# Two edits of a fused forward and backward kernel: block 3 of the first norm turned by DMA, and one pair of loads held on an earlier product

## Chip, cores and metric

The kernel runs on one core of a Trainium2 chip. The metric is the device time of one execution in microseconds (us): the median of several executions, lower is better. All times of single instructions below come from one profiled execution.

## The reference, cut to what matters

Four residual layers, A, B, A, B (numbered l = 0 to 3 in the kernel), and then the gradients of all six inputs by reverse differentiation. S = 2048 rows, D = 512, 32 heads of 16, F = 1376, everything in bfloat16.

```
x = x + A(layernorm(x));  x = x + B(layernorm(x));  x = x + A(layernorm(x));  x = x + B(layernorm(x))
A: q, k, v = h @ wqkv;  pq, pk = phi(q), phi(k)                  # phi(t) = t + 1 where t > 0, else exp(t)
   kv = sum over s of pk^T v;  z = sum over s of pk;  o = (pq @ kv) / (pq . z);  return o @ wo
B: return (sigmoid(h @ w_gate) * (h @ w_up)) @ w_down
outputs: x and the gradients of x, wqkv, wo, w_gate, w_up, w_down
```

The edits touch the layernorm in front of the first layer A (l = 0) and the backward pass of both layers A (l = 2, which comes first, and l = 0, which comes last).

## The kernel before

**Tiling.** The 2048 rows are 16 tiles of 128 rows (`st`), four to a block (`b` = 0 to 3, `j` the tile in the block). Each tile of x stays in SBUF through the whole program. A matmul contracts over partitions, so most stages need the rows both as they are (`h`) and turned (`hT`, features on partitions).

**The first norm** is `LN.one` for l = 0 (L276 to L298). For each tile it takes the statistics on DVE and POOL, writes `h` on DVE (L288), turns it with four TensorE transposes against the identity into a PSUM bank `T_ps` (L292), and copies the bank to `hT` on ScalarE: one tile at a time in block 0 (L296), two tiles at a time in blocks 1 to 3 (L298). At the end of a block `h` is stored from POOL's queue (L317), and `hT` is put on a list of stores for SP's queue (L319, L221). The later norms (l = 1 to 3) turn their rows by DMA transposes from SBUF to SBUF on SP's queue (L314).

**The stage around it** is `AFwd.first` (L483). It walks over the 16 tiles: it asks the norm to be six tiles ahead (L501), computes the keys of a later tile (`keys`, L464: `k_ps` on TensorE from `hT`, then ScalarE and DVE make `pk_t`), for some tiles a pair of query products from a block's `hT` (`query`, L522), and then the sums `E_ps` (L512, from `h` and `pk_t`) and `z_ps` (L515). `hT` of tiles 12 and 13 is first read by the thirteenth key product, that of tiles 14 and 15 by the fifteenth. Finished pairs of `pk_t` are turned by DMA transposes on SP (L478); the weights of layer B are loaded on SP, each held on a certain `pk_t` (L425 to L429).

**The backward of a layer A** is `a_bwd1` and then `a_bwd2`. `a_bwd1` (L1021) has per block b: four products `dq_ps` (L1071) from the turned gradient `gaT_t`, each followed by two "fill" products, DVE and POOL work (`soft`, L1049), and sixteen sums `CT_ps` (L1046) that read `qn_l` of the block. The inputs of block b come from DRAM over SP's queue: `loads(b)` are two loads of 512 KB (`qp_l` L1035 and `dqT_t` L1036), `rows_n(b)` is one (`qn_l` L1041). `loads(0)` and `rows_n(0)` are written first, `loads(1)` is held on the last of twelve fill products (L1063, L1064), and the later ones on a ScalarE copy of the block before (L1083).

**The fill** (`Fill`, L227) is a weight gradient of layer 3 that is cut into 11 groups of 16 products (L250) and put in wherever TensorE would wait. The input of a group is one DMA transpose of 512 KB from DRAM (`hf_t`, L238); two buffers take turns, and the load of the next group is written ahead of a group's fourth product. The last-but-one `a_bwd1` (l = 2) starts with product 0; the last one (l = 0) starts with the sixteenth product of group 7, so that the load for group 9 is written ahead of its fifth product, and its buffer comes free with its first.

**Order.** The program is written in one order; a planner then gives each engine, and each engine's DMA queue, an order of its own: what its estimate says is ready goes first, and among what is ready, what was written first. An engine's queue is then worked off strictly in that order. So in the trace the load of group 1 of the fill is issued at 493.39 us, ahead of loads that were written before it (501.64 us). `held` adds a wait; it does not place the instruction.

Of the kernel before, what the change touches and what calls it, by code (L numbers as in the profile page):

```python
# [22 lines left out]
NDC = D // P  # L23
# [23 lines left out]
def by_tile(ap2d, st, n):  # L47
    return ap2d[rows(st, n), :].rearrange("(n p) d -> p n d", p=P)


def by_chunk(ap2d, b):

    return ap2d[:, b * SB:(b + 1) * SB].rearrange("(c p) s -> p c s", p=P)
# [101 lines left out]
def flat(t):  # L155
    return t[:].rearrange("p a b c -> p (a b c)") if len(t.shape) == 4 else t[:].rearrange("p a b -> p (a b)")
# [37 lines left out]
def mm4(k, out, lhs, rhs, n=NDC):  # L194
    for c in range(n):
        i = k.nc.tensor.matmul(out, lhsT=lhs(c), rhs=rhs(c), start=(c == 0), stop=(c == n - 1))  # L196
    return i


def after(k, second, first, cls=None):  # L200

    k.tc.add_manual_dep(second.ins, first.ins.name,
                        mybir.DependencyInfo(cls or mybir.DependencyClass.NoSync, mybir.DependencyReason.DATA),
                        reason="order")


def held(k, first, *loads):
    for ld in loads:
        after(k, ld, first, mybir.DependencyClass.Sync)


def store_turned(k, dst, t):

    flush_turned(k)
    k.turned.append((dst, t))
# [47 lines left out]
class LN:  # L263
# [12 lines left out]
    def one(self, st):  # L276
        k, nc, l = self.k, self.k.nc, self.l
        b, j = divmod(st, NB)
        if j == 0:
            self.h[b] = k.p_h.tile([P, NB, D], BF16, name="h_t", tag="h_t")  # L280
            self.hT[b] = k.p_hT.tile([P, NB, NDC, P], BF16, name="hT_t", tag="hT_t")
        if l == 0:
            if st == 0:
                self.stats(0)
            if st + 1 < NST:
                self.stats(st + 1)
            mean, rstd = self.got.pop(st)
            self.applied.append(nc.vector.tensor_scalar(self.h[b][:, j, :], narrow(k, st), mean, rstd, ALU.subtract, ALU.mult))  # L288
            if j % 2 == 0:
                self.tp = k.bank([P, 2 * NDC, P], BF16, name="T_ps")  # L290
            for c in range(NDC):
                t = nc.tensor.transpose(self.tp[:, j % 2 * NDC + c, :], self.h[b][:, j, c * P:(c + 1) * P], k.ident[:])  # L292
                if st == 2 and c == 0:
                    after(k, t, k.last_key)
            if b == 0:
                nc.scalar.copy(self.hT[b][:, j], self.tp[:, j % 2 * NDC:j % 2 * NDC + NDC, :])  # L296
            elif j % 2:
                nc.scalar.copy(self.hT[b][:, j - 1:j + 1].rearrange("p a c q -> p (a c) q"), self.tp[:])  # L298
        elif j % 2:

            rstd = k.rstd[l][:, st - 1:st + 1]
            neg = k.small.tile([P, 2], F32, name="ln_neg", bufs=8)
            nc.scalar.mul(neg[:], k.sums[st // 2][:], -1.0 / D)
            ss = k.small.tile([P, 2], F32, name="ln_ss")
            for i in range(2):
                nc.scalar.activation(self.h[b][:, j - 1 + i, :], k.xs[st - 1 + i][:], ACT.Square, bias=neg[:, i:i + 1],
                                     accum_out=ss[:, i:i + 1])
            nc.gpsimd.tensor_scalar(rstd, ss[:], 1.0 / D, EPS_LN, ALU.mult, ALU.add)
            nc.gpsimd.tensor_tensor(rstd, rstd, k.neghalf[:], ALU.pow)
            for i in range(2):  # L310
                nc.vector.tensor_scalar(self.h[b][:, j - 1 + i, :], k.xs[st - 1 + i][:], neg[:, i:i + 1],
                                        rstd[:, i:i + 1], ALU.add, ALU.mult)
            if b or l == 2:
                nc.sync.dma_start_transpose(out=self.hT[b][:, j - 1:j + 1].rearrange("p a c q -> p (a c) q"),  # L314
                                            in_=self.h[b][:, j - 1:j + 1, :].rearrange("p a d -> p (a d)"))
        if j == NB - 1:
            k.st.dma_start(out=by_tile(k.sv[l]["h"], b * NB, NB), in_=self.h[b][:])  # L317
            if l % 2 == 0:
                store_turned(k, k.sv[l]["hT"][b], self.hT[b])  # L319
# [25 lines left out]
def narrow(k, st):  # L345

    return k.xs[st][:].bitcast(BF16)[:, D:2 * D]
# [673 lines left out]
def a_bwd1(k, l, big, ph1, p_dq):  # L1021
    nc, sv, A = k.nc, k.sv[l], k.A[l]
    MT = k.p_mt.tile([P, NDC, D], BF16, name="MT_l", tag="MT")
    nc.sync.dma_start(out=flat(MT), in_=k.wT[4 if l else 5][:])
    dzp = big.tile([P, NDC, NBLK], F32, name="dzp")
    CT_ps = [k.bank2([P, D], F32, name="CT_ps") for _ in range(NDC)]
    late, gs, dqTs, qps, qns = [], k.early, [], [], {}

    def loads(b):

        if b % 2 == 0:
            qps.append(k.p_sh.tile([P, 2, NDC, SB], BF16, name="qp_l", tag="sh"))
        dqTs.append(p_dq.tile([P, NDC, SB], BF16, name="dqT_t"))
        half = NDC * SB
        lds = (nc.sync.dma_start(out=flat(qps[-1][:, b % 2]), in_=sv["qr"][b][:, 0:half]),  # L1035
               nc.sync.dma_start(out=flat(dqTs[b]), in_=sv["qr"][b][:, half:2 * half]))  # L1036
        return lds

    def rows_n(b):
        qns[b] = big.tile([P, NDC, NB, P], BF16, name="qn_l", tag=f"big{b % 2}")  # L1040
        return nc.sync.dma_start(out=flat(qns[b]), in_=sv["qn"][b])  # L1041

    def sums(b, g_t, qn):
        for jc in range(NDC):
            for j in range(NB):
                nc.tensor.matmul(CT_ps[jc][:], lhsT=g_t[:, j, jc * P:(jc + 1) * P], rhs=qn[:, :, j, :],  # L1046
                                 start=(b == 0 and j == 0), stop=(b == NBLK - 1 and j == NB - 1))

    def soft(b, dc, dq, u_t, qp, dqT):  # L1049
        t_ps = k.bank([P, SB], F32, name="t_ps")  # L1050
        nc.tensor.matmul(t_ps[:], lhsT=k.bdmask[:], rhs=u_t[:], start=True, stop=True)
        w_t = ph1.tile([P, SB], BF16, name="w_t", bufs=3)
        nc.vector.scalar_tensor_tensor(w_t[:], t_ps[:], A["nz"][:, dc:dc + 1], dq[:], ALU.mult, ALU.add)
        nc.gpsimd.tensor_tensor(dqT[:, dc, :], w_t[:], dqT[:, dc, :], ALU.mult)
        nc.vector.scalar_tensor_tensor(u_t[:], t_ps[:], -1.0, qp[:, dc, :], ALU.mult, ALU.mult,
                                       accum_out=dzp[:, dc, b:b + 1])
        if dc == NDC - 1:
            k.st.dma_start(out=by_chunk(sv["dqT"], b), in_=dqT[:])

    loads(0)  # L1060
    rows_n(0)
    gs.append(a_grads(k, 2))
    k.fill.step(12)  # L1063
    held(k, k.fill.last, *loads(1))  # L1064
    for b in range(NBLK):
        g_t, gT = gs[b]
        qp, dqT = qps[b // 2][:, b % 2], dqTs[b]
        qn = qns[b]
        for dc in range(NDC):
            ps = k.bank([P, SB], F32, name="dq_ps")  # L1070
            mm4(k, ps[:], lambda c: MT[:, c, dc * P:(dc + 1) * P], lambda c: gT[:, :, c, :])  # L1071
            dq = ph1.tile([P, SB], BF16, name="dq_sb", bufs=3)
            k.mark = nc.scalar.copy(dq[:], ps[:])
            u_t = ph1.tile([P, SB], BF16, name="u_t", bufs=3)
            nc.vector.tensor_tensor(u_t[:], dq[:], qp[:, dc, :], ALU.mult)
            late.append((b, dc, dq, u_t, qp, dqT))
            k.fill.step(2)
            if len(late) > 2:
                soft(*late.pop(0))
            if (b, dc) == (0, 1):  # L1080
                gs.append(a_grads(k, 3))
            if dc == 1 and b + 1 < NBLK:
                held(k, k.mark, rows_n(b + 1), *(loads(b + 2) if b + 2 < NBLK else ()))  # L1083
                if b == 1 and l == 2:
                    held(k, k.mark, nc.sync.dma_start(out=flat(k.woT), in_=k.wT[0][:]),
                         *(nc.sync.dma_start(out=flat(k.wqkvT[:, NDC * i:NDC * i + NDC, :]), in_=k.wT[1 + i][:])
                           for i in range(3)))
        sums(b, g_t, qn)
    while late:
        soft(*late.pop(0))  # L1090


    CT = big.tile([P, NDC, D], BF16, name="CT_t", tag="big0")
    for jc in range(NDC):
        nc.scalar.copy(CT[:, jc, :], CT_ps[jc][:])
    k.st.dma_start(out=sv["CT"][:].rearrange("(c p) d -> p c d", p=P), in_=CT[:])
    return CT, dzp, dqTs
# [246 lines left out]
```

## Time and profile before

| | |
|---|---|
| median of 4 executions | 1090.32 us (1088.72 to 1092.0) |
| the profiled execution | 1092.0 us, of them 1090.3 us from the first to the last instruction |
| TensorE busy | 1062.0 us, 97% of the span |
| DVE, ScalarE, POOL busy | 51%, 41%, 28% |
| first norm's transposes on TensorE (L292) | 64, 7.4 us busy, 5.8 to 35.4 us |
| copies of two turned tiles on ScalarE (L298) | 6, 1010 ns each |
| DMA transposes of key pairs, 256 KB (L478) | 16; to landing 3.1, 4.4, 8.5 us (least, median, most) |
| loads qp_l, dqT_t, qn_l, 512 KB each | to landing 6.4, 7.2, 6.3 us (median) |
| fill loads hf_t, 512 KB, turned | 11; to landing 7.2 us (median) |
| l = 2 `a_bwd1` | its products start at 501.45 us |
| l = 0 `a_bwd1` | its products start at 738.95 us |

How to read it: TensorE is busy nearly all of the span, so a wait of TensorE is the place where time can be gained or lost, and the other engines and the queues count where they make TensorE wait. In a timeline of an engine, a line gives the start, the duration, the engine, the source line, the operation, what it writes and reads, how often, and in brackets how long the engine had stood idle and what ended it. The start of TensorE's next line is the better measure of a matmul's cost, since matmuls overlap. "SPq" is SP's queue, whose instructions only issue DMAs.

### The profile page before, as it was taken

The page shows a single profiled execution, that of the slowest core. Times are in us where ns is not written, and L with a number is a line of the kernel's source. Part 1 is how long each engine was busy: PE and PEld are TensorE (multiplying, and loading weights), DVE is VectorE, ACT ScalarE, POOL GpSimd, SP SyncE. Part 2 cuts the span into 40 slices and gives each one's busy share as a digit, 9 for nine tenths or more (in the row PEclk, how much of TensorE's full clock was granted, in tenths as well). Part 3 has the DMA queues.
Part 4 walks back from the last instruction along what each step waited for, and adds up shares of the span by engine and source line. Part 5 has one row for each costly group of instructions (what it writes and reads, how often), then busy time and mean ns, then how long its engine had stood idle before and what let it go on. Part 6 is the DMA issues. An engine that isn't in the chain of part 4 may idle for free.

```text
span 1090.3 us, 15262 instructions
## 1 busy us (share of the span) xinstructions
PE 1062.0 (97%) x5448; PEld 495.0 (45%) x5448; DVE 551.4 (51%) x1029; ACT 444.9 (41%) x930; POOL 306.5 (28%) x410
## 2 busy tenths in 40 slices
PE   6989999999999999999899999999999999999998
PEld 3444444444444444444344444444444444465443
DVE  7687765668935443545676534557877100001110
ACT  3477686448736464533234533434336100000010
POOL 5334443104643434231532200003623200001110
PEclk9999999999999999999999999999999999999999
DMA  9988988679999999899997888869989996499991
GB/s 270 274 230 274 293 220 246 190 191 256 269 237 221 261 185 271 193 221 210 340 312 214 233 274 240 238 184 251 355 233 341 259 248 154 123 213 237 260 223 41
DMA packets 401869, 258.50 MB, mean 237 GB/s; under 512 B 308720, under 2 KB 371472, under 8 KB 400512
## 3 DMA queue, kind: packets, MB, share of 16 engines
q1 hardware_dynamic: 386608, 208.12, 77.2%
q0 software_dynamic: 15184, 49.39, 13.0%
q8 instruction: 43, 0.70, 0.3%
q14 instruction: 34, 0.28, 0.1%
HBM read 76.19 MB, written 106.79 MB: 168 GB/s over the span
## 4 chain that ended last, share of the span: by engine, by line
PE 68%; DMA 2%; ACT 1%; DVE 1%; issue 1%; POOL 1%; SPq 0%; ACTq 0%; DVEq 0%; POOLq 0%
PE dw_ps L1288 19%; PE dh_ps L848 7%; PE dh_ps L942 7%; PE dhh_ps L196 6%; PE dh_ps L1127 5%; PE y_ps L196 4%; PE dw_ps L1306 3%; PE u_ps L196 3%; PE g_ps L196 3%; PE dh_ps L1118 3%; PE dpk_ps L196 2%; PE CT_ps L1046 2%; PE fill_ps L250 2%; PE dq_ps L196 2%; DMA hf_t<-sv_hhT 1%
## 5 line engine op out<-in xcount | busy, mean ns | idle before, releaser
L1288 PE MATMUL dw_ps<-set_t,rows_t 128*128 128x512 bf16 (+1 forms) x1024 | 204.4, 362 | 0.0
L1288 PEld LDWEIGHTS <-rows_t 128*128 128x128 bf16 x1024 | 100.1, 98 | 103.7
L672 POOL TENSOR_TENSOR sd_t<-sd_t,hh_t 128x512 bf16<-128x512 bf16 x68 | 80.7, 1187 | 138.3 <-DVE hh_t L667 76.0
L1207 DVE CAST dw_new<-dw_ps 128x512 bf16<-128x512 f32 (+1 forms) x20 | 12.4, 654 | 186.5 <-PE dw_ps L1288 186.1
L1207 ACT CAST dw_new<-dw_ps 128x512 bf16<-128x512 f32 (+1 forms) x20 | 10.5, 561 | 225.7 <-PE dw_ps L1288 188.1
L912 ACT ACTIVATE t_sb<-dh_ps,rstd 128x512 f32<-128x512 f32 x64 | 43.5, 681 | 138.4 <-PE dh_ps L848 75.7
L196 PE MATMUL g_ps<-hT_t,wg 128*128 128x512 bf16 (+1 forms) x360 | 90.7, 374 | 1.7 <-DMA hT_t<-h_t 1.3
L196 PE MATMUL u_ps<-hT_t,wu 128*128 128x512 bf16 (+1 forms) x360 | 90.7, 374 | 0.9 <-DVE hh_t L667 0.7
L196 PE MATMUL dhh_ps<-gT_t,wdT 128*128 128x512 bf16 x352 | 90.5, 379 | 0.8 <-ACT dhh_t L969 0.8
L942 PE MATMUL dh_ps<-wuT,dd_t 128*128 128x512 bf16 x176 | 66.7, 379 | 0.0
L942 PE MATMUL dh_ps<-wgT,dd_t 128*128 128x512 bf16 x176 | 66.7, 379 | 0.0
L667 DVE SCALAR_TENSOR_TENSOR hh_t<-sd_t,u_ps 128x512 bf16<-128x512 bf16 x88 | 59.7, 680 | 11.4 <-ACT sd_t L666 10.6
L665 ACT ACTIVATE g_ps<-g_ps 128x512 f32<-128x512 f32 x88 | 53.0, 603 | 27.2 <-PE g_ps L196 27.0
L1208 POOL DMA_DIRECT2D out_dram<-dw_new x36 | 19.3, 543 | 156.5 <-DVE dw_new L1207 152.5
L666 ACT ACTIVATE sd_t<-g_ps,onef 128x512 bf16<-128x512 f32 x88 | 60.8, 693 | 2.7
L971 DVE TENSOR_TENSOR dd_t<-dhh_t,sh_t 128x1024 bf16<-128x1024 bf16 x44 | 30.0, 691 | 58.7 <-ACT dhh_t L969 54.4
L757 DVE TENSOR_TENSOR sd_t<-dhh_t,sd_t 128x1024 bf16<-128x1024 bf16 x44 | 30.4, 690 | 48.8 <-POOL sd_t L672 45.9
L196 PEld LDWEIGHTS <-wu 128*128 128x128 bf16 x360 | 35.2, 98 | 42.1 <-issue 1.5
L196 PEld LDWEIGHTS <-wg 128*128 128x128 bf16 x360 | 34.4, 98 | 42.5 <-issue 2.2
L196 PEld LDWEIGHTS <-wdT 128*128 128x128 bf16 x352 | 34.4, 98 | 42.3 <-issue 1.3
L848 PEld LDWEIGHTS <-sd_t 128*128 128x128 bf16 x352 | 34.5, 98 | 41.5
L942 PEld LDWEIGHTS <-dd_t 128*128 128x128 bf16 x352 | 34.4, 98 | 41.5
(166 smaller groups left out, 1843.0 us busy)
## 6 DMA issues: line engine op xcount, KB each, us to landing
sv_sd<-sd_t SPq DMA_DIRECT2D x22, 512.0 KB, 3.5
sv_ddT<-dd_t SPq DMA_DIRECT2D x40, 256.0 KB, 4.9
sv_h<-h_t POOLq DMA_DIRECT2D x16, 512.0 KB, 4.7
sv_qr<-pe_t POOLq DMA_DIRECT2D x16, 512.0 KB, 4.3
sh_t<-sv_sd SPq DMA_DIRECT2D x8, 1024.0 KB, 6.7
rows_t<-sv_h SPq DMA_DIRECT2D x16, 512.0 KB, 6.9
sv_ddN<-nat_t SPq DMA_DIRECT2D x15, 512.0 KB, 4.6
set_t<-sv_ddN SPq DMA_DIRECT2D x12, 512.0 KB, 6.0
```

The costliest lines, as they stand in the source:

```text
L196: i = k.nc.tensor.matmul(out, lhsT=lhs(c), rhs=rhs(c), start=(c == 0), stop=(c == n - 1))
L665: nc.scalar.activation(g_ps[:], g_ps[:], ACT.Tanh, scale=-0.5)
L666: nc.scalar.activation(sd[:, 0, :], g_ps[:], ACT.Identity, bias=k.onef[:], scale=-1.0)
L667: nc.vector.scalar_tensor_tensor(hh[:], sd[:, 0, :], 0.5, u_ps[:], ALU.mult, ALU.mult)
L672: nc.gpsimd.tensor_tensor(sd[:, 1, :], sd[:, 1, :], hh[:], ALU.mult)
L848: k.nc.tensor.matmul(dh[j][:], lhsT=dds[fc][:, a, rows(j)], rhs=(k.wuT, k.wgT)[a][:, fc, :], start=(a == fc == 0), stop=(a == 1 and fc == ...
L912: nc.scalar.activation(t_sb[:], dh_ps, ACT.Identity, scale=rstd, accum_out=c1[:])
L942: nc.tensor.matmul(acc[b][j][:], lhsT=dd[:, a, rows(j)], rhs=(k.wuT, k.wgT)[a][:, fc, :], start=(fc == 0 and a == 0), stop=(fc == NFC - 1 ...
L1118: nc.tensor.matmul(dh[j][:], lhsT=dqTs[b][:, c, rows(j)], rhs=k.wqkvT[:, c, :], start=(c == 0), stop=False)
L1127: nc.tensor.matmul(dh[j][:], lhsT=lhs(j, c), rhs=rhs(c), start=False, stop=stop and c == NDC - 1)
L1288: k.nc.tensor.matmul(ps[ic][:, 0:w], lhsT=h_m[:, ic * P:(ic + 1) * P], rhs=t_m, start=(m == 0), stop=(m == n - 1))
L1306: k.nc.tensor.matmul(p[0:r, :], lhsT=t[:, f:f + r], rhs=g_t, start=(i == 0 and st == 0), stop=(i == len(srcs) - 1 and st == NST - 1))
```

## The change

The first edit is in `LN.one`. For the tiles of block 3 alone the four TensorE transposes per tile, the PSUM bank and the ScalarE copies are left out, and after each second tile one DMA transpose from SBUF to SBUF is issued on SP's queue, in the form that the later norms use. The second edit is in `a_bwd1`, which is run for l = 2 and for l = 0: `loads(1)` is written after the second instead of after the twelfth of the first fill products, and is held on the second. The number of products does not change.

```
             self.applied.append(nc.vector.tensor_scalar(self.h[b][:, j, :], narrow(k, st), mean, rstd, ALU.subtract, ALU.mult))
-            if j % 2 == 0:
+            if b < 3 and j % 2 == 0:
                 self.tp = k.bank([P, 2 * NDC, P], BF16, name="T_ps")
-            for c in range(NDC):
+            if b >= 3:
+                if j % 2:
+                    nc.sync.dma_start_transpose(out=self.hT[b][:, j - 1:j + 1].rearrange("p a c q -> p (a c) q"),
+                                                in_=self.h[b][:, j - 1:j + 1, :].rearrange("p a d -> p (a d)"))
+            for c in range(NDC if b < 3 else 0):
                 t = nc.tensor.transpose(self.tp[:, j % 2 * NDC + c, :], self.h[b][:, j, c * P:(c + 1) * P], k.ident[:])
...
-            elif j % 2:
+            elif b < 3 and j % 2:
                 nc.scalar.copy(self.hT[b][:, j - 1:j + 1].rearrange("p a c q -> p (a c) q"), self.tp[:])
...
     loads(0)
     rows_n(0)
     gs.append(a_grads(k, 2))
-    k.fill.step(12)
+    k.fill.step(2)
     held(k, k.fill.last, *loads(1))
+    k.fill.step(10)
```

## The prediction, made before the changed kernel was run

> **What bounds the kernel now.** I read the page first: TensorE's share and the chain that ended last.
>
> ```profile
> PE 1062.0 (97%) x5448; PEld 495.0 (45%) x5448; DVE 551.4 (51%) x1029; ACT 444.9 (41%) x930; POOL 306.5 (28%) x410
> ...
> PE 68%; DMA 2%; ACT 1%; DVE 1%; issue 1%; POOL 1%; SPq 0%; ACTq 0%; DVEq 0%; POOLq 0%
> ```
>
> TensorE is the bound nearly everywhere. Time can be won only where TensorE works on something that goes away, or waits; the chain's 2% of DMA are such waits. So I went to the three places that the change touches, with TensorE's timeline, SP's queue, and windows with clock and DMA share. First the first norm, on TensorE:
>
> ```profile
> 30.98 0.33 PE L292 MATMUL T_ps<-ident,h_t 128*128 128x128 bf16 x3
> 31.14 1.03 PE L196 MATMUL k_ps<-wkvo,hT_t 128*128 128x512 bf16 x4
> ...
> 35.21 0.38 PE L292 MATMUL T_ps<-ident,h_t 128*128 128x128 bf16 x4
> 35.43 1.03 PE L196 MATMUL k_ps<-wkvo,hT_t 128*128 128x512 bf16 x4
> ...
> 40.81 1.02 PE L196 MATMUL k_ps<-wkvo,hT_t 128*128 128x512 bf16 x4
> ```
>
> From 30 to 56 us TensorE has no gap over 0.15 us, so here its own work counts. Four transposes take 0.22 us (35.21 to 35.43), not the 0.38 of their pipelined duration. The last 16 of the 64 are block 3's: five at 26.96, three at 30.98, four each at 32.97 and 35.21. The product at 40.81 is the thirteenth of the keys, the first reader of tiles 12 and 13; that of tiles 14 and 15 starts at 46.19.
>
> Then the `a_bwd1` of l = 2. SP's queue, TensorE, and windows (their last two figures are granted clock, and DMA share with GB/s):
>
> ```profile
> 502.63 0.33 SPq L1041 DMA_DIRECT2D qn_l<-sv_qn  x1
> 504.23 0.32 SPq L1035 DMA_DIRECT2D qp_l<-sv_qr  x1
> ...
> 514.08 7.38 SPq L238 DMA_TRANSPOSE hf_t<-sv_hhT  x1
> ...
> 522.18 0.38 SPq L1041 DMA_DIRECT2D qn_l<-sv_qn  x1
> ```
>
> ```profile
> 524.44 1.03 PE L196 MATMUL dq_ps<-gaT_t,MT_l 128*128 128x512 bf16 x4
> ...
> 528.69 0.59 PE L1046 MATMUL CT_ps<-qn_l,ga_t 128*128 128x512 bf16 x1 [2.57 <-DMA qn_l<-sv_qn]
> 529.07 1.91 PE L196 MATMUL dq_ps<-gaT_t,MT_l 128*128 128x512 bf16 x4
> ```
>
> ```profile
> 502.00:503.00 1.00, 1.00 (x7) 0.43 (x5) 0.54 (x1) 0.63 (x3) 0.00 (x0) 1.00 0.38 70
> ...
> 504.00:505.00 1.00, 1.00 (x6) 0.49 (x5) 0.76 (x2) 0.96 (x2) 0.00 (x0) 1.00 0.62 213
> ...
> 528.00:530.00 2.00, 1.31 (x4) 0.48 (x4) 0.00 (x0) 0.00 (x0) 1.70 (x2) 0.67 1.02 391
> 530.00:535.00 5.00, 5.00 (x20) 2.08 (x19) 2.64 (x7) 1.17 (x2) 1.56 (x3) 0.79 1.01 398
> ```
>
> The longest wait after the start is here: 2.57 us for the third `qn_l`, issued only at 522.18 because the loads ahead of it crowd the queue (DMA share about 1 from 505 us on, the fill's load alone 7.38 us in issue). It costs more than itself: the clock is granted at 0.67 and 0.79 behind it, so that the same four products take 1.91 instead of 1.03. Lost by that: (1 - 0.67) x 2 + (1 - 0.79) x 5 = 1.7 us.
>
> Last the `a_bwd1` of l = 0, SP and then TensorE:
>
> ```profile
> 739.15 0.34 SPq L1036 DMA_DIRECT2D dqT_t<-sv_qr  x1
> 739.58 3.56 SPq L238 DMA_TRANSPOSE hf_t<-sv_hhT  x1
> 743.19 0.57 SPq L1035 DMA_DIRECT2D qp_l<-sv_qr  x1
> ```
>
> ```profile
> 746.48 0.82 PE L250 MATMUL fill_ps<-gf_t,hf_t 128*128 128x512 bf16 x3 [1.10 <-DMA hf_t<-sv_hhT]
> ```
>
> Here `loads(1)` (743.19) already stands behind the fill's load, SP being busy with that until 743.14; TensorE waits 1.10 us for that fill load, and the clock stays at 1.00.
>
> **Edit 1, part by part.** Removed: 16 transposes. The five at 26.96 stand ahead of a wait for `pk_t` (0.51 us, ended at 30.01), which grows by what they leave: nothing gained. The other eleven: 0.16 + 0.22 + 0.22 = 0.60 us on the path. The two ScalarE copies (1.01 us each, at 31.34 and 35.63) lie just ahead of the exponentials of two keys; without them those come sooner, so DVE's `pk_t` doesn't eat the 0.60. Bounds 0.3 (the next `pk_t` is late by half) to 0.9 (all 16 x 0.055). I take **-0.6**.
>
> Added: two transposes of 256 KB on SP. `h` of tiles 12 and 13 is done at 26.06, of 14 and 15 at 29.0 (DVE's timeline). The nearest rows are the 16 of the key pairs: 1.2 to 3.9 us of SP each, landing after 3.1 to 8.5 us; the slowest of this size in the trace took 10.0. Issued by 31 us they land by 36 to 41, against needs at 40.2 and 45.6: hidden. Behind them on SP are the key pairs' transposes and the weight loads; these move by up to 8 us, and the first reader of the nearest (`wg`, issued 29.99, landing 8.5 us later) is at 72.38. The store of `hT` (issued 39.92) now waits for the second transpose on SP, with `wu` behind it, landing at 49 and first read at 74.0. The DMA share is near 1 up to 70 us, but 0.00 from 76 to 78: the added 0.5 MB has been worked off by then. If this cover is gone, see rival 3. I take **0** for all added work.
>
> VectorE: DVE Perf Modes, "The three transpose paths", speaks against this edit: 1309 ns for a 128x128 turn by DMA against 390 on TensorE, with TensorE to be used where PSUM will do. In this trace the two are 0.055 us in the stream and 3.1 to 8.5 us for eight such turns. By the page's figure, an estimate, eight turns take 10.5 us and both pairs 21: from 26.1 to 47, 1.5 us too late for the second. The rows decide for me.
>
> **Edit 2, l = 2.** The second product ends at about 501.9; SP is busy with `qn_l` until 502.96. So `loads(1)` goes out at 503.05 instead of 504.23, 1.2 us sooner. Its own readers did not wait. What it does is start the crowd earlier: the turned gradients behind it are held to 505.2 by ScalarE's casts, but their bytes, and all up to the third `qn_l`, follow a megabyte that is further along. The gain at 528.69 is at least the share left idle at 504 to 505, 0.38 us, and at most the whole lead, 1.2; below nothing is excluded, as the bytes and their order are the same. Middle: **-0.8**. The wait is then 1.8 us. A wait of 1.10 (746.48) left the clock alone, one of 2.57 halved it, and so did one of 2.52 at 13.9 us; 1.8 is nearer to 1.10, so I let the halved clock go too: **-1.7**. Between none and all: 0 to -1.7.
>
> TensorE: Matmul & The Clock Gate, "Part 1", puts the drop after an idle window of some 3.4 us, so that 2.57 us should cost nothing beyond itself. By that rule the 1.7 would not be there to win; the windows above show that it is.
>
> **Edit 2, l = 0.** `loads(1)` and the fill's load come ready 0.22 us apart (first and second product), while SP issues the load at 739.15. If their order stays, nothing moves: **0**. If it turns, rival 2.
>
> **Sum.** 1092.0 - 0.6 - 0.8 - 1.7 = **1088.9** for an execution like the profiled one. That one was the slowest of four, 1.7 above the median of 1090.32: about the price of one halved-clock window, which other executions may not have had. For these, 1090.3 - 0.6 - 0.8 = 1088.9. Both say 1088.9, with 1087.7 to 1090.4 by the bounds; that is 0.13% below the median, and 0.2% (2.2 us) is about what a measurement of this kernel can tell from no change.
>
> **Rivals.**
> 1. **The whole lead comes through.** All that is queued up to the third `qn_l` lands 1.2 to 2.5 us sooner, so the wait at 528.69 shrinks to nothing much and no execution has the halved window. For: the DMA share is about 1 all the way. Against: the casts hold the queue at 505.2. 1092.0 - 0.6 - (1.2 to 2.5) - 1.7 = 1087.2 to 1088.5; about **1087.3**.
> 2. **Slower: the two loads pass the fill's load at l = 0.** SP is held 0.38 us by the load at 739.15. If the planner sees it held until the second product is done (0.43 us after the phase begins), `loads(1)`, now written first, goes first: from that point on this decides. The fill's load then stands behind 1 MB more, 2.4 to 2.8 us at 375 to 437 GB/s. The wait of 1.10 becomes 3.7 and surely halves the clock: +2.6 + 1.7, **1093.2**. Less if the planner, seeing the fill late, puts the sums `CT_ps` into the hole: then 1089 to 1092.
> 3. **Block 3 comes late.** If the transposes are planned behind those at 31.76 and 36.24, SP is free for them at 38.3, and they land at 41.4 to 48: 1 to 7 us of waiting. Against: `h` is ready before these key pairs. About **1092**.
>
> **Chances.** Forecast 0.40 (0.10 of it below 1088.1, by the bounds and the executions), rival 1 0.28 (all faster), rival 2 0.22 (0.06 of it within 0.2%), rival 3 0.10 (0.06 within). Faster 0.38, within 0.2% 0.42, slower 0.20. The range goes from rival 1 with half a microsecond of luck to rival 2's price: 1086.4 to 1093.4; the forecast's own is 1087.7 to 1090.4.
>
> **What would show it.** 48 transposes at L292 and four copies of two tiles; two `hT_t<-h_t` transposes before 32 us, landing before 41, and no wait of a `k_ps` for them; the thirteenth key product at 40.2. The second `qp_l` of l = 2 within 1.5 us of the first product, the wait for the third `qn_l` under 2 us and the clock at 1.00 behind it. At l = 0 the fill's load still ahead of `qp_l`, its wait still about 1.1. A wait of 3 us there, or a `k_ps` waiting for DMA, makes the prediction wrong.

## The result, and the profile after

The changed kernel takes 1093.82 us (median of 43 executions), the kernel before 1090.61 us (64 executions beside it); the ratio is 1.0031, with a 95% interval of 1.0018 to 1.0043. So it is slower by 0.3%, where 1088.9 us, 0.13% faster, had been forecast; the measured time lies just above the upper end of the range (1093.4). The profiled execution of the changed kernel took 1094.41 us with a span of 1092.7 us, against 1092.0 and 1090.3 before: 2.4 us more span to be explained. Line numbers after the first edit are higher by 4 (L292 is L296, L1041 is L1045), and by 5 after the second.

The page of the changed kernel: TensorE's busy time, the chain that ended last, and the group of the fill products with the idle time ahead of them.

```profile
PE 1061.8 (97%) x5432; PEld 493.8 (45%) x5432; DVE 552.9 (51%) x1029; ACT 443.6 (41%) x928; POOL 306.2 (28%) x410
...
PE 69%; DMA 2%; DVE 2%; ACT 1%; issue 0%; POOL 0%; SPq 0%; ACTq 0%; DVEq 0%; POOLq 0%
...
L250 PE MATMUL fill_ps<-gf_t,hf_t 128*128 128x512 bf16 (+1 forms) x176 | 48.6, 383 | 6.3 <-DMA hf_t<-sv_hhT 6.2
```

Sixteen TensorE instructions are gone (5432 instead of 5448), and one wait stands out: 6.2 us for a fill load, in a kernel whose TensorE hardly waits otherwise. Next the first norm, on SP and then on TensorE:

```profile
26.81 1.48 SPq L293 DMA_TRANSPOSE hT_t<-h_t  x1
...
31.18 2.95 SPq L293 DMA_TRANSPOSE hT_t<-h_t  x1
```

```profile
24.31 0.39 PE L296 MATMUL T_ps<-ident,h_t 128*128 128x128 bf16 x4
...
39.68 1.02 PE L196 MATMUL k_ps<-wkvo,hT_t 128*128 128x512 bf16 x4
```

The last transposes on TensorE are those at 24.31; the two DMA transposes landed at 30.53 and 36.84 us, and the thirteenth key product (39.68, before 40.81) waits for neither. By the start of `a_bwd1` of l = 2 the kernel is ahead by 0.82 us (its first product at 500.63 instead of 501.45).

Then `a_bwd1` of l = 2: SP's queue, TensorE where the wait was, and two windows (granted clock, DMA share and GB/s at the end).

```profile
501.48 0.32 SPq L1045 DMA_DIRECT2D qn_l<-sv_qn  x1
501.90 0.37 SPq L1039 DMA_DIRECT2D qp_l<-sv_qr  x1
...
512.32 6.29 SPq L238 DMA_TRANSPOSE hf_t<-sv_hhT  x1
...
519.32 0.40 SPq L1045 DMA_DIRECT2D qn_l<-sv_qn  x1
```

```profile
525.38 0.38 PE L1050 MATMUL CT_ps<-qn_l,ga_t 128*128 128x512 bf16 x1
525.68 1.02 PE L196 MATMUL dq_ps<-gaT_t,MT_l 128*128 128x512 bf16 x4
```

```profile
528.00:530.00 2.00, 2.00 (x11) 0.88 (x9) 2.00 (x6) 0.59 (x1) 1.68 (x3) 1.00 1.03 416
530.00:535.00 5.00, 5.00 (x25) 2.28 (x24) 3.80 (x6) 0.71 (x2) 1.73 (x3) 1.00 1.03 414
```

`qp_l` follows `qn_l` at once (501.90), and the third `qn_l` is issued at 519.32 instead of 522.18. The first `CT_ps` that reads it has no wait in brackets, and the clock is at 1.00 behind it: 2.57 us of waiting and 1.7 us of halved clock are gone. A later product (535.51, before 540.40) is ahead by 4.89 us, that is 4.07 more than at the start of this stage.

Last `a_bwd1` of l = 0, where the time is lost: SP, TensorE, windows.

```profile
733.53 0.34 SPq L1040 DMA_DIRECT2D dqT_t<-sv_qr  x1
733.96 0.38 SPq L1039 DMA_DIRECT2D qp_l<-sv_qr  x1
734.39 0.42 SPq L1040 DMA_DIRECT2D dqT_t<-sv_qr  x1
734.87 6.61 SPq L238 DMA_TRANSPOSE hf_t<-sv_hhT  x1
```

```profile
739.59 2.11 PE L1050 MATMUL CT_ps<-qn_l,ga_t 128*128 128x512 bf16 x9
747.85 0.61 PE L250 MATMUL fill_ps<-gf_t,hf_t 128*128 128x512 bf16 x1 [6.15 <-DMA hf_t<-sv_hhT]
748.27 0.61 PE L1055 MATMUL t_ps<-u_t,bdmask 128*128 128x512 bf16 x1
```

```profile
742.00:746.27 4.27, 0.00 (x0) 0.00 (x0) 0.02 (x1) 1.04 (x3) 0.54 (x1) 1.00 1.34 143
746.27:749.68 3.41, 1.83 (x5) 0.71 (x6) 0.75 (x2) 0.00 (x0) 0.00 (x0) 0.50 0.90 248
749.68:753.10 3.42, 3.42 (x10) 1.21 (x9) 2.22 (x5) 0.59 (x1) 1.51 (x2) 0.50 1.05 294
```

The order on SP has turned: the two loads (733.96, 734.39) stand ahead of the fill's load (734.87), which before stood ahead of them. It holds SP for 6.61 us instead of 3.56 and lands 12.94 us after its issue (747.81) instead of 6.85. The planner did put nine of the sums `CT_ps` into the hole (739.59), and still TensorE stands for 6.15 us, and for 6.83 us the clock is halved. That is no accident of one execution: in a second profile of the changed kernel TensorE waits 4.71 us at the same place, and the mean granted clock of an execution (in which a halved stretch anywhere counts) is under 1.00 in all 44 of the changed kernel, while in 67 of 133 of the kernel before (those beside the experiments) it is 1.00.

**The account.** From the issue of the load `dqT_t` at the start of this stage (739.15 before, 733.53 after) to the same product further on (755.45 and 757.45) it is 16.30 us before and 23.92 after: +7.62. Of that the wait is 6.15 - 1.10 = 5.05, and the clock (753.10 - 747.85) x 0.5 = 2.63. All in all, on the span: -0.82 (up to l = 2, the first norm's part), -4.07 (l = 2), -0.73 (two waits of 0.40 and 0.35 us for `dhh_t` at 623.84 and 626.94 that are not there after; no part of either edit explains them), +7.62 (l = 0), +0.39 (the end) = +2.39.

### The profile page after: what moved, and what is told of

It is laid out like the page before. It is cut to its first block, busy times and chain, and to the rows that moved or that the text cites. A ratio compares the mean times of both kernels' runs of the same rounds, so it can differ in the third digit from the quotient of the medians.

```text
span 1092.7 us, 15237 instructions
## 1 busy us (share of the span) xinstructions
PE 1061.8 (97%) x5432; PEld 493.8 (45%) x5432; DVE 552.9 (51%) x1029; ACT 443.6 (41%) x928; POOL 306.2 (28%) x410
## 4 chain that ended last, share of the span: by engine, by line
PE 69%; DMA 2%; DVE 2%; ACT 1%; issue 0%; POOL 0%; SPq 0%; ACTq 0%; DVEq 0%; POOLq 0%
PE dw_ps L1293 19%; PE dh_ps L852 7%; PE dh_ps L946 7%; PE dhh_ps L196 6%; PE dh_ps L1132 5%; PE y_ps L196 4%; PE dw_ps L1311 3%; PE u_ps L196 3%; PE g_ps L196 3%; PE fill_ps L250 3%; PE dh_ps L1123 3%; PE CT_ps L1050 2%; PE dq_ps L196 2%; PE dpk_ps L196 2%; DMA hf_t<-sv_hhT 1%; DMA qn_l<-sv_qn 1%
## 5 line engine op out<-in xcount | busy, mean ns | idle before, releaser
L250 PE MATMUL fill_ps<-gf_t,hf_t 128*128 128x512 bf16 (+1 forms) x176 | 48.6, 383 | 6.3 <-DMA hf_t<-sv_hhT 6.2
```

What stands on the lines that cost most here:

```text
L250: self.last = nc.tensor.matmul(ps[0:w, :], lhsT=t[:, st, 0:w], rhs=self.g[st // NB][:, st % NB, :], start=(st == 0), stop=(st == NST - 1))
```

## The experiments

Theory A, from the two traces: the edits are separate, edit 1 and edit 2 at l = 2 win a little, and all of the loss comes from the order on SP at l = 0. The rivals: B, the two added DMA transposes crowd a queue; C, what is won at l = 2 is given back at l = 0 because the traffic there doesn't come sooner; C2, the early hold costs as such, whichever load goes first; D, E, G, H are named where they were tried. A ratio below is to the kernel before on the same chip, with its 95% interval.

### Which part loses

One part of the change at a time. Edit 1 alone leaves `loads(1)` as before; edit 2 alone leaves `LN.one` as before; the other two have edit 1 and

```
-    k.fill.step(2)
+    k.fill.step(2 if l == 2 else 12)        # edit 2 at l = 2 alone;  for l = 0 alone: l == 0
     held(k, k.fill.last, *loads(1))
-    k.fill.step(10)
+    k.fill.step(10 if l == 2 else 0)
```

**Edit 1 alone.** 

> Edit 1 alone; the loads of both passes stand as before. Theory A (the two edits are separate; the loss arises in edit 2 at l = 0 by the order on SP): 0.5 to 0.9 us faster than before; the wait for the third qn_l at about 528 stays at 2.6 us, the wait for the fill's load in a_bwd1(0) at 1.1. Rival B (the two DMA transposes of block 3 crowd a queue, and that brings the loss): slower than before by 1 us or more, with new TensorE waits for DMA.

**Edit 2 alone.** 

> Edit 2 alone, in both passes; block 3 turned on TensorE as before. A: the changed kernel's time plus about 0.7, so 3 to 4.5 us slower than before; no wait over 1 us at l = 2, one of about 6 us for the fill's load at l = 0, with the halved clock behind it. B: within 1 us of before.

**Edit 1, and edit 2 at l = 2.** 

> Edit 1, and edit 2 at l = 2 alone; at l = 0 the loads stand as before. A: 4 to 5 us faster than before (0.7 of edit 1, 2.6 of the wait that goes, up to 1.7 of the clock behind it); the wait for the fill's load at l = 0 stays at 1 to 1.5 us. Rival C (what is won at l = 2 is given back, since the fill's load at l = 0 is bound by traffic that doesn't come sooner): that wait grows to 4 to 6 us and the time is within 2 us of before.

**Edit 1, and edit 2 at l = 0.** 

> Edit 1, and edit 2 at l = 0 alone; at l = 2 the loads stand as before, so this pass begins nearly at its old time. A: the wait for the fill's load is about 6 us and halves the clock behind it: 6 to 7.5 us slower than before, and 7 to 8 slower than edit 1 alone. C: the wait stays under 3 us and the time is within 2 us of before.

| kernel | median, us | ratio | wait for the third `qn_l`, l = 2 | wait for the fill's load, l = 0 |
|---|---|---|---|---|
| edit 1 alone | 1089.78 | 0.9993 (0.9979 to 1.0008) | 1.73 | 0.83 |
| edit 2 alone | 1095.53 | 1.0048 (1.0033 to 1.0063) | 0.36 | 5.46 |
| edit 1, edit 2 at l = 2 | 1089.93 | 0.9993 (0.9973 to 1.0014) | none | 0.68 |
| edit 1, edit 2 at l = 0 | 1096.63 | 1.0066 (1.0043 to 1.0088) | 0.94 | 4.88 |

B falls: with edit 1 alone nothing is lost. C falls: with edit 2 at l = 2 alone the wait at l = 0 stays at 0.68, and without it, at the old time, the wait is there all the same (4.88). The loss goes with edit 2 at l = 0: 1096.63 - 1089.78 = 6.85 us, where A expected 7 to 8; edit 2 alone, at 5.2 us by its ratio, costs somewhat more than the 3 to 4.5 expected. What A had wrong is the worth of l = 2: not 4 to 5 us, but in this pair nothing that can be told from zero. Two lines show why. TensorE with edit 1 alone:

```profile
527.27 0.38 PE L1050 MATMUL CT_ps<-qn_l,ga_t 128*128 128x512 bf16 x1 [1.73 <-DMA qn_l<-sv_qn]
```

and with edit 1 and edit 2 at l = 2:

```profile
800.37 2.98 PE L196 MATMUL dpk_ps<-haT_l,Wp_t 128*128 128x512 bf16 x13 [1.66 <-DMA haT_l<-sv_hT]
```

With the order of before, the wait at l = 2 was 1.73 us in this execution and did not touch the clock: the profiled execution of before, with 2.57 and a halved clock, had been an unlucky one. And in the other kernel a new wait of 1.66 us had come up later. Both kernels were run again side by side.

**Edit 1 alone, again.** 

> Edit 1 alone once more, as the yardstick for the next one on the same chip. Both theories: 0.5 to 0.9 us faster than before, and a wait of 0.9 to 2.6 us for the third qn_l.

**Edit 1 and edit 2 at l = 2, again.** 

> Edit 1 and edit 2 at l = 2 alone, once more. A: no wait, or one under 1 us, for the third qn_l, and 1 to 2 us faster than edit 1 alone; the wait of 1.7 us for haT_l at 800 us, seen in the first of these runs, was that execution's and isn't there. Rival E: the wait for haT_l is there again, and the time is that of edit 1 alone within 0.5 us.

1088.01 us (0.9997, 0.9973 to 1.0021) and 1087.41 us (0.9969, 0.9947 to 0.9991). The second of them, on TensorE:

```profile
525.27 0.38 PE L1050 MATMUL CT_ps<-qn_l,ga_t 128*128 128x512 bf16 x1 [0.18 <-DMA qn_l<-sv_qn]
...
740.31 0.82 PE L250 MATMUL fill_ps<-gf_t,hf_t 128*128 128x512 bf16 x3 [1.09 <-DMA hf_t<-sv_hhT]
```

The wait at 800 us was not there again: it had been that execution's, and E (a new wait takes its place) falls. But edit 1 alone had no wait over 0.15 us for the third `qn_l` this time, so there was little to win. Over all profiles of this study the five with the old order at l = 2 waited 2.57, 1.73, 0.94, 0.93 and under 0.15 us there, 1.2 on average; the thirteen with the new one none to 1.43, 0.3 on average. So edit 2 at l = 2 takes some 0.9 us off that wait on average. What that is worth in time stays open: the two pairs of medians differ by +0.15 and -0.6 us (the ratios by 0 and 0.28%, with intervals that overlap), but with edit 2 at l = 0 in both, the change (1.0031) stands 0.35% below the kernel without edit 2 at l = 2 (1.0066, six executions).

### The order, or the early hold?

```
     k.fill.step(2)
-    held(k, k.fill.last, *loads(1))
-    k.fill.step(10)
+    second = k.fill.last
+    k.fill.step(3 if l == 0 else 0)         # the fill's load is written in here
+    for ld in loads(1):
+        held(k, second, ld)
+        if l == 0:
+            after(k, ld, k.fill.ld)         # an order alone, no wait
+    k.fill.step(7 if l == 0 else 10)
```

> Both edits, and at l = 0 the loads are still held on the second fill product, but are written behind the fill's load, so that SP issues that one first. Theory A (what costs is that the fill's load stands behind the loads' 1 MB): as with edit 2 at l = 2 alone, 0 to 1.5 us faster than before, and a wait of 0.5 to 1.5 us for the fill's load. Rival C2 (the early hold itself costs, since the loads' bytes run beside the fill's, whichever goes first): a wait of 3 to 6 us, 3 to 6 us slower than before.

Measured: 1089.41 us, 0.9979 (0.9958 to 1.0001). SP, and TensorE's wait:

```profile
734.72 4.21 SPq L238 DMA_TRANSPOSE hf_t<-sv_hhT  x1
738.99 0.57 SPq L1039 DMA_DIRECT2D qp_l<-sv_qr  x1
```

```profile
742.27 0.82 PE L250 MATMUL fill_ps<-gf_t,hf_t 128*128 128x512 bf16 x3 [1.75 <-DMA hf_t<-sv_hhT]
```

The hold on the second product is the changed kernel's; only the order on SP is swapped (by what is written first, and by `after`), and the loss is gone: 2.3 us faster than before, with an interval from 4.6 faster to zero, where A expected 0 to 1.5. C2 falls for the time; the wait of 1.75 us is above the 1.5 that A allowed, but 1.67 was also seen with edit 1 alone (again), so it is within what executions differ by. That the order decides is shown.

### What the place costs

At l = 0 one load goes ahead of the fill's load, and the other is held on the twelfth product (`loads` now takes the names of what it loads):

```
+    held(k, k.fill.last, *loads(1, ("dqT",) if l == 0 else ("qp", "dqT")))
     k.fill.step(10)
+    if l == 0:
+        held(k, k.fill.last, *loads(1, ("qp",)))
```

> Both edits, but at l = 0 only one of the two loads (dqT_t, 0.5 MB) goes ahead of the fill's load, the other is held on the twelfth product as before. A, by bytes: half of the delay, so a wait of about 3 us (between 0.8 of edit 1 alone and 4.9 to 6.2 with both loads ahead), 1.5 to 4 us slower than before. Rival D (any load ahead costs all of it, as the fill's turned load is only taken up when what is ahead has drained): a wait of 4.5 us or more, 3 to 6 us slower.

Or the first halves of both loads go ahead (two transfers of 0.25 MB), the second halves later:

> The changed kernel, but at l = 0 only the first half of each of the two loads goes ahead of the fill's load (two transfers of 0.25 MB), the other halves are held on the twelfth product as before. By bytes: as with one whole load ahead, a wait of 2 to 3.2 us, within 1 us of before. By the number of transfers ahead: as with both whole loads, a wait of 4.5 us or more, 3 us or more over before's.

The changed kernel was also profiled once more:

> The changed kernel once more, for the spread of one execution's wait. All theories: a wait of 4.8 to 6.3 us for the fill's load at l = 0, the fill's load landing 4.9 to 6.3 us after the load ahead of it.

Measured: 1090.23 us, 0.9992 (0.9973 to 1.0011), with one load ahead; 1091.26 us, 1.0019 (1.0007 to 1.0031), with two halves. The changed kernel's second profile had a wait of 4.71 us, just under what all theories gave. The waits of the first two, in this order:

```profile
742.06 0.39 PE L250 MATMUL fill_ps<-gf_t,hf_t 128*128 128x512 bf16 x1 [2.56 <-DMA hf_t<-sv_hhT]
```

```profile
743.16 0.61 PE L250 MATMUL fill_ps<-gf_t,hf_t 128*128 128x512 bf16 x1 [3.56 <-DMA hf_t<-sv_hhT]
```

A table of the landings, all from the traces (us). "Ahead" is what SP issued just before the fill's load, the stage's first `dqT_t` (0.5 MB) included, which stands there in every kernel; the second column runs from that load's issue to the landing of the last one ahead, the third from there to the fill's load's landing. (In the kernels left out, the third column is 2.8 to 3.2 us with 0.5 MB ahead, and 5.5 with edit 2 alone, which has 1.5 MB.)

| kernel | ahead, MB | ahead landed after | fill's load after that | TensorE waited |
|---|---|---|---|---|
| before | 0.5 | 4.15 | 3.13 | 1.10 |
| edit 1 alone | 0.5 | 3.99 | 3.02 | 0.83 |
| fill's load first | 0.5 | 4.84 | 3.09 | 1.75 |
| one load ahead | 1.0 | 6.02 | 3.15 | 2.56 |
| two halves ahead | 1.0 | 6.80 | 3.37 | 3.56 |
| edit 1, edit 2 at l = 0 | 1.5 | 8.07 | 4.94 | 4.88 |
| the change | 1.5 | 8.11 | 6.17 | 6.15 |
| the change, again | 1.5 | 8.05 | 4.78 | 4.71 |

So the delay has two parts. The megabyte ahead takes 4.0 us (8.07, less the mean of 4.15 and 3.99), which is 262 GB/s, where the prediction had priced it at 375 to 437 GB/s: rates that the trace before reaches in other stretches (375 at l = 2 about 505 us, 437 at l = 0 only from 756 us on), while in this place, from 739.15 to 743.30 and from there to 746.43, the DMA engines moved 165 and 306 GB/s before the change too. It goes roughly by bytes (2 us for 0.5 MB); that the two halves took 0.8 us more than one whole load is no more than the rows with 0.5 MB differ by among themselves (3.99 to 4.84). D (any load ahead costs all) falls, though A's time was missed as well: 0.9 us faster than before, where 1.5 to 4 slower had been expected. The halves meet neither reading (3.56 us, and 2.1 us slower than before, where bytes gave 2 to 3.2 and within 1 us, and transfers 4.5 or more and 3 us or more). The second part is 1.7 to 3.1 us that come on top, in this table only with 1.5 MB ahead. Of the sum (14.28 - 7.28 = 7.0 us in the change) the wait's growth is 5.05; the other 1.95 us are filled, by the nine `CT_ps` sums (2.11 us) that the planner put there.

### The second part

Theory G: turned loads of other data (the fourth block's gradients, issued from 742.20 on) run beside the fill's and slow it. H: a turned load that has stood behind so much needs that long by itself. It took three steps, as each turned load that was put off let the next one in. The gradients' turned loads two chunks later, then one block later, both by the place of one call:

```
-            if (b, dc) == (0, 1):
+            if (b, dc) == (0, 1 if l == 2 else 3):          # then: ((0, 1) if l == 2 else (1, 0))
                 gs.append(a_grads(k, 3))
```

> The changed kernel, but at l = 0 the casts and turned loads of the fourth block's gradients are written two query chunks later. In the changed kernel, and with edit 2 at l = 0 alone, the fill's load landed 6.2 and 4.9 us after the load ahead of it, elsewhere 3.1 to 3.3; in both the gradients' turned loads were out by then. Theory G (6 us of delay are 4 for the bytes ahead and 2 for turned loads that run beside the fill's): it lands 3 to 3.5 us after the load ahead of it, the wait is 2.5 to 4 us, and the time 2 to 3 us less than the changed kernel's, 0 to 1.5 us slower than before. Rival H (all of it is the bytes ahead): the wait stays at 4.9 to 6.2 us, 3 us or more slower than before.

> The changed kernel, with the turned loads of the fourth block's gradients at l = 0 written one block later and behind the fill's next load, so that none is out while the fill's load is. (Two chunks later, they had still gone out 2 us after the load ahead had landed.) Theory G (2 us of the 6 are turned loads beside the fill's): the fill's load lands 3 to 3.6 us after the load ahead of it, the wait is 2.5 to 3.5 us, the time 0 to 1.5 us over before's. Rival H (a turned load that has stood behind two others needs 5 us or more by itself): 4.9 us or more from landing to landing, wait 4.5 to 6.2, 3 us or more over before's.

and then these, the fill's next load, and the first turned load of the weight gradients, all held on a product of the fill's next group:

> The changed kernel, with every turned load that could run beside the fill's load at l = 0 held until a product of the fill's next group: the gradients' of the fourth block, the fill's next, and the first of the weight gradients'. (With the gradients' alone put off, the fill's next one had gone out in their place, 1.5 us after the load ahead had landed.) Only untouched straight loads run beside it. Theory G: 3 to 3.6 us from the landing ahead to that of the fill's load, wait 2.5 to 3.5 us. Rival H: 4.9 us or more, wait 4.5 to 6.2.

Measured: 1093.36 us, 1.0024 (1.0009 to 1.0040), wait 4.77, 5.11 us from landing to landing; 1093.18 us, 1.0038 (1.0023 to 1.0053), 4.96 and 5.15; 1094.58 us, 1.0032 (1.0013 to 1.0050), 6.14 and 6.13. The first two settle nothing, as in the first the gradients' loads came only 2 us later and in the second the fill's next load took their place at 742.18. The third does: SP and TensorE,

```profile
735.28 6.63 SPq L238 DMA_TRANSPOSE hf_t<-sv_hhT  x1
741.97 0.58 SPq L1049 DMA_DIRECT2D qn_l<-sv_qn  x1
742.59 0.45 SPq L1043 DMA_DIRECT2D qp_l<-sv_qr  x1
743.08 0.43 SPq L1044 DMA_DIRECT2D dqT_t<-sv_qr  x1
753.43 0.37 SPq L1120 DMA_DIRECT2D ha_l<-sv_h  x1
```

```profile
748.26 0.61 PE L252 MATMUL fill_ps<-gf_t,hf_t 128*128 128x512 bf16 x1 [6.14 <-DMA hf_t<-sv_hhT]
```

After 735.28 no turned load is issued until 754.76, and the wait is as long as ever. G falls. H's numbers came, but H doesn't hold either: in the version with the whole change and one product more, which follows below, another turned load of 512 KB (`set_t`, 735.26) stands behind the same 1.5 MB and lands 3.2 us after it (741.47 and 744.70).

Both theories leave out POOL's queue, on which the fill's last finished result is stored beside the fill's load (`sv_wd<-wd_part`, 256 KB, 64 packets of 4 KB; issued at 736.07 in the change, 741.69 before). In all seven traces with 4.8 us or more from landing to landing, the store's first packet moved when 19 to 26% of the turned load's 2048 packets had; in the eight with 2.8 to 3.4 us, and in the one with `set_t`, when 95 to 98% had. In the first microsecond after the last landing ahead, SP's queue moved 1126 packets before, 1134 in the one with `set_t`, and 346 in the change, where 34 of POOL's queue moved beside them. So the second part goes with this store running through the turned load, and not with the bytes ahead as such. That it is the cause is not shown, as no run moved the store alone, and why it starts there is open.

### A version that beats both

If the place of the fill's load is the cause, the loads may go early once it has left. Its buffer comes free with the last product of the fill's group 7, which was the first product of `a_bwd1` at l = 0. One fill product more in the feed-forward backward ahead brings that forward:

```
-                        k.fill.step(5 if b == 0 else 3)
+                        k.fill.step(5 if b == 0 else 4 if (l, b, fc) == (1, NBLK - 1, 2) else 3)
```

This was run with edit 1 and edit 2 at l = 2 alone, with the whole change, and with edit 1 alone:

> Edit 1, edit 2 at l = 2 alone, and one fill product more in the feed-forward backward ahead (47 become 48), so that the buffer of the fill's next load comes free before a_bwd1(0) starts and SP issues that load earlier. A: no wait for the fill's load at l = 0, 0.7 us less than with edit 2 at l = 2 alone, so 1 to 2.5 us faster than before. Rival E (the time comes back as another wait for DMA behind it, as 1.7 us at 800 us did in the run before with edit 2 at l = 2 alone): within 0.7 us of before.

> As the kernel with one fill product more, but with edit 2 whole: at l = 0 the loads are held on the second product again. The fill's load has left before them. A: harmless now, within 1 us of the kernel with one more product, and 4 to 6 us faster than the same without it (the changed kernel's own place of the loads). C2: a wait of 3 us or more at l = 0, 3 us or more slower than the kernel with one more product.

> Edit 1 and one fill product more ahead, with edit 2 nowhere. Theory A (edit 2 at l = 2 wins the wait for the third qn_l, 0.9 to 2.6 us, and nothing gives it back once the fill's load is out of the way): 1 to 2 us slower than the kernel with one more product and edit 2 at l = 2, that is 1 to 2 us faster than before; a wait of 0.9 us or more at about 526. Rival E (what is won at l = 2 is given back at l = 0): the same as that kernel within 0.5 us.

| with one product more | median, us | ratio |
|---|---|---|
| edit 1, edit 2 at l = 2 | 1087.71 | 0.9976 (0.9953 to 1.0000) |
| the whole change | 1086.99 | 0.9968 (0.9947 to 0.9989) |
| edit 1 alone | 1087.93 | 0.9974 (0.9959 to 0.9990) |

The whole change with that one product moved has the lowest median of the study: 0.3% faster than before, where without it the change is 0.3% slower. The fill's load now goes out at 706.30 us and lands at 711.64. SP and TensorE of this kernel at l = 0:

```profile
734.36 0.38 SPq L1039 DMA_DIRECT2D qp_l<-sv_qr  x1
734.79 0.42 SPq L1040 DMA_DIRECT2D dqT_t<-sv_qr  x1
735.26 5.90 SPq L1271 DMA_TRANSPOSE set_t<-sv_ddT  x1
```

```profile
739.77 1.03 PE L250 MATMUL fill_ps<-gf_t,hf_t 128*128 128x512 bf16 x4
```

The loads stand where the change puts them; behind them is now a turned load that nobody needs yet, which still holds SP for 5.90 us; and the products at 739.77, the first that read the new fill load, have no wait. So C2 falls once more, and the size is 0.63% between the two (1.0031 to 0.9968), 6.8 us, more than the 4 to 6 that A gave. Of the last run, A had expected 1 to 2 us more than with edit 2 at l = 2; it was 0.2 us. In this pair too the worth of edit 2 at l = 2 is not to be told from nothing. E's "the same within 0.5 us" is what was measured, but its reason (what is won at l = 2 is given back at l = 0) is not seen: a late `qn_l` at l = 0 is waited for in both kernels, 1.09 us at 762.31 with edit 1 alone and 1.20 us at 759.22 with edit 2 at l = 2.

## Why the prediction was wrong

Step by step, as it was put.

- **"So I take -0.6"** for edit 1: right as far as the runs can tell. Between 30 and 53 us, where block 3's transposes stood, the lead over the kernel before grows by 0.83 us, and it is 0.82 at the next stage that the change touches, within the bounds of 0.3 to 0.9; the two timings of edit 1 alone are 0.9993 and 0.9997, both with intervals that hold -0.06% and zero. "I take 0 for all added work" is right too: the transposes landed at 30.5 and 36.8 us, within the 36 to 41 forecast or sooner, and no key product waited.
- **"Middle: -0.8"** and **"-1.7"** at l = 2: the direction is right. In the pair of profiled executions more came true (2.57 and 1.7), which is rival 1. Against other executions, less: the average wait there was 1.2 us, and of the five executions with the old order only that one had the halved clock. The text saw this ("which other executions may not have had") and still built the main term on the one that was profiled.
- **"If their order stays, nothing moves: 0"** at l = 0: this is the step that failed. The order turned. What decides it stood ahead of the prediction: the planner fixes the order by its own estimate, and between loads that are ready it takes what was written first; the two loads are now written after the second product of the stage, the fill's load for group 9 ahead of its fifth. Which of the two, the estimate or the written order, turned them here, no run separates. The prediction knew this as rival 2, but made it hang on 0.43 us against 0.38, took the trace's times for the planner's, and gave it 0.22. In the trace after, the fill's load would have been ready sooner (first product done at 733.71; second 733.93; SP free at 733.87): what was ready on the chip did not decide. The run with the fill's load put first on SP, and the same hold, took the loss away.
- **Rival 2's price, "+2.6 + 1.7"**: mis-sized. The wait grew by 5.05, not 2.6, and the clock cost 2.6, not 1.7: 7.6 in place of 4.3. The first part because 1 MB took 4 us here, not 2.4 to 2.8 (the rate was read from other stretches of the trace); the second because the load then needed 1.7 to 3.1 us more, in all seven traces with the store from POOL's queue running through it, though that cause was not tested by itself; the clock because the wait was long enough for two halved windows. The sums `CT_ps` did go into the hole, which the text took to bring the price down to 1089 to 1092, and filled 1.95 us of it. That rival 2's 1093.2 is so near the measured 1093.82 is luck: in the pair of profiles the larger gain at l = 2 (4.07 for 2.5) made up for half of the larger loss at l = 0 (7.6 for 4.3).
- **Rival 3**, block 3 late: didn't happen.
- The range's ends lie a little outside of what the text derives them from: half a microsecond off rival 1's 1087.2 is 1086.7, not 1086.4, and rival 2's price is 1093.2, not 1093.4. The measured time is above both.
- The sign that the prediction had named ("a wait of 3 us there") is the one that came.

## What to carry to other kernels

When a load is moved forward, write down for each queue which instruction it will now be written ahead of, and ask whether that one has a reader that waits; in a queue that is worked off in order, a change from "behind" to "ahead" can cost more than the whole gain, and it is decided when the queue is planned, not by a fraction of a microsecond in the trace. Price the bytes ahead at the rate of that stage, with turned loads in it, and not at the best rate of the trace, and look at what the other queues send at that moment. And before a wait of one profiled execution is made a term of the sum, ask how much of it the median has: here it was twice the average.

## What the runs showed of the hardware

**The clock goes by windows of 3.41 us on a fixed grid.** In one execution the halved stretches start whole numbers of 3.413 us apart: 13.28 and 528.70 before (151 of them), 746.27 and 1091.02 after (101), 14.09 and 744.54 in the kernel without turned loads beside (214). Each of the 18 profiles was cut into its windows, from where its clock is on record (9.9 to 20.2 us after the start) to the last one whole within the span. A full window with 2.05 us or more of standing was followed by a halved one, with 1.75 or less it was not; of the two between, 1.76 us was (12.23, the fill's load first) and 1.80 us was not (1079.33, behind the last product of edit 1 alone, again). A halved window with 0.97 us or more was followed by another halved one, with 0.61 or less by a full one. So what a stall costs depends on where the grid cuts it: 5.46 us with edit 2 alone fell into three windows, as 1.59, 3.41 and 0.45, and only the last of them was halved; 4.77 us with the gradients' loads two chunks later fell into two, as 2.15 and 2.62, and the second and the one behind it were halved. This is why the 6.15 us of the change cost two windows: one full of standing, then 1.58 us more in the halved one. The Trainium skill (TensorE: Matmul & The Clock Gate, "Part 1") has the window's length and that it runs free of the kernel; its drop after one idle window is more than was needed here, where 2.05 us of standing in a window were always enough.

**Issuing the fill's turned load held SP about until what was ahead of it had landed.** In all rows of the table above, SP was through with it 0.1 to 0.2 us before the last load ahead landed (739.22 and 739.32 with edit 1 alone, 741.48 and 741.64 in the change). So here the 3.5 or 6.6 us of issue go with the drain of the queue, and whatever stands behind on SP shares that wait. It is no rule without exception: of the change's eleven fill loads ten kept to it within 0.5 us, but the last was through in 1.52 us (750.08), 3.5 us before the load ahead of it landed (755.14).
